# Row maxima of an attention unit: transposed by VectorE in squares of 32 instead of by a matmul

## The chip, the cores and the metric

The kernel runs on one core of a Trainium2 chip. The metric is the device time of one execution in microseconds (us); "before" and "after" are each given as the median over several executions. A core has a matrix engine (TensorE, PE in the profile; its weight loads are listed apart as PEld), a vector engine (VectorE, DVE), an engine for activation functions (ScalarE, ACT), a general one (GpSimd, POOL) and a queue engine (SyncE, SP), which here issues all transfers. SBUF is the core's working memory of 128 partitions; PSUM holds eight banks into which matmuls write; DRAM is the memory outside the core.

## The reference

```python
xn = _layernorm(x)                                   # x: 1 x 2048 x 512, fp32
qkv = (xn @ wqkv)                                    # 32 heads of 16
scores = einsum("bhqd,bhkd->bhqk", q, k) * 16 ** -0.5
p = softmax(scores)                                  # over 2048 keys
s = einsum("bhqk,bhkd->bhqd", p, v) ... @ wo         # attention, 512 x 512 output weights
h = relu(xn @ w1 + b1) ** 2                          # 512 -> 1792
g = silu(h @ w2 + b2)                                # 1792 -> 512
out = x + s * g
```

Everything is fp32. The softmax of the reference subtracts the maximum of each score row before the exponential. The kernel does that too, and the change is in how these maxima get to the place where they are subtracted.

## The kernel before

fp32 operands are split into a high and a low part, and a product is the sum of three matmuls. The 32 heads are taken four at a time (eight "quads"), and the 2048 queries in four chunks of 512. One quad with one chunk is a *unit*; there are 32 units (`NU`). For a unit the kernel does two things, far apart in time.

*Maxima.* `max_mm` (L288 to L310) computes, for one head, 128 queries and 512 keys, the scores in one PSUM bank (matmul L300), and VectorE reduces the bank to one column of maxima (L308). A unit has 4 heads x 4 blocks of 128 queries x 4 chunks of 512 keys, that is 64 such matmuls and 64 reductions. The banks come from the pool `pm`, which has three: a matmul can start when the reduction of the matmul three places before it has let go of its bank. When the 64 are done, `max_end` (L314) reduces the 64 columns to 16 (L326), one per head and block of queries, partitions being queries: a tile `m4` of 128 x 16. It notes the unit in `late`, due two steps on.

*Shift.* `shift_due` (L330) calls `shift(u)` (L334) when the unit is due. The maxima have to become rows: for head and query block a row of 128 values. Before, a matmul against the identity does it (L336, a PE transpose of 128 x 16 into 16 x 128), which takes one of the three `pm` banks. VectorE reads the bank twice: it writes the negated maxima as a high part (L338) and the remainder as a low part (L339) into the tile `sh` of 16 partitions. The inner function `keep` writes the two halves to the DRAM tile `sh_d[u]` by two transfers (L345), and `back`, through `shift_rows` (L367, transfer L368), reads them into rows 48 and 49 of each half of the unit's query tiles `qe`. The key tiles have ones in these rows, so the score matmul itself subtracts the maximum.

*Use.* `exp_mm` (L1245) makes the scores of 128 keys by 512 queries (matmul L1258) and ScalarE takes the exponential (L1264); `pv_step` multiplies with the values (matmuls L375, in `pv_mm`) and accumulates over the 16 blocks of keys of a unit. One block of keys of one unit is a *step*; there are 512 steps. When a unit ends, `evac` starts a chain of small works over the next steps, among them three GpSimd instructions one behind the other (L413, L414, L415 in `evac_norm`).

The MLP (`mlp_tasks`) and the output product are generators whose matmuls are laid between those of the attention: `slot` (L1298) and `long_slots` (L1337) write out, matmul by matmul, which follows which. Two matmuls of 64 rows each run side by side in the upper and the lower half of the array, so their order alternates between the halves. The L336 transpose and the L375 matmuls use all 128 rows. From L1417 on the order on all engines is that of the program text: on VectorE the reductions of the maxima come in the order of their matmuls, and the shift's instructions stand between two of them, at the end of a slot. SP too takes its transfers in the order of the text and stands still when the next one has to wait; `keep` is put one step, `back` at least two steps behind `shift` (`later`, L181, due by `run_waiting`, L185). `back` is due 14 steps ahead of the first step of its unit or, where the shift comes after that, two steps behind the shift. In the stage before the loop (`first`, L1104) TensorE, VectorE, ScalarE and GpSimd keep the order of the text.

The loop has three kinds of stretches around a shift: slots of a single step (2.9 us each), pairs of steps in which long blocks of MLP matmuls stand (5.5 us a pair, `long_slots` in its first form), and the same blocks cut at each step (2.1 and 3.6 us in turn, its second form). The rows of the next sections are from these.

Of the kernel before, what the change touches and what calls it, by code (L numbers as in the profile page):

```python
# [8 lines left out]
F32 = mybir.dt.float32  # L9
F32R = mybir.dt.float32r  # L10
AF = mybir.ActivationFunctionType
ALU = mybir.AluOpType
# [4 lines left out]
P = 128  # L17
# [9 lines left out]
NU = NQ * 4  # L27
# [13 lines left out]
def kernel(  # L41
# [11 lines left out]
    nc = tc.nc  # L53
# [3 lines left out]
    dram = ctx.enter_context(tc.tile_pool(name="dram", bufs=1, space=DRAM))  # L57
    q_d = [dram.tile([2, P, S], F32, name=f"q_d{m}") for m in range(4)]
    k_d = [dram.tile([2, P, S], F32, name=f"k_d{m}") for m in range(4)]
    sh_d = [dram.tile([4, 2, 512], F32, name=f"sh_d{u}") for u in range(NU)]  # L60
    r_d = [dram.tile([4, 512], F32, name=f"r_d{u}") for u in range(NU)]
    on_d = [dram.tile([2, P, S], F32, name=f"on_d{k}") for k in range(KO)]
    xn_d = dram.tile([2, P, KO, S], F32, name="xn_d")
# [5 lines left out]
    ident = const.tile([P, P], F32, name="ident")  # L69
# [26 lines left out]
    with ExitStack() as ph:  # L96
        kp = ph.enter_context(tc.tile_pool(name="kp", bufs=1))
        sp = ph.enter_context(tc.tile_pool(name="asp", bufs=2))
        pe = ph.enter_context(tc.tile_pool(name="pe", bufs=3, space=PSUM))
        pm = ph.enter_context(tc.tile_pool(name="pm", bufs=3, space=PSUM))  # L100
# [27 lines left out]
        mxs = {}  # L128
# [52 lines left out]
        def later(n, fn):  # L181
            waiting.append((now[0] + n, fn))
# [147 lines left out]
        def shift_due():  # L330
            if late and late[0][0] <= now[0]:
                shift(late.pop(0)[1])

        def shift(u):  # L334
            pt = pm.tile([P, 512], F32, name="pm_t")
            nc.tensor.transpose(pt[:16, :P], mxs[u], ident)  # L336
            sh = sp.tile([16, 2, P], F32R, name="sh", bufs=1)
            nc.vector.tensor_scalar(sh[:, 0], pt[:16, :P], -1.0, None, op0=ALU.mult)  # L338
            nc.vector.scalar_tensor_tensor(  # L339
                sh[:, 1], pt[:16, :P], -1.0, sh[:, 0].bitcast(F32),  # L340
                op0=ALU.mult, op1=ALU.subtract,
            )
            def keep():
                for i in range(2):
                    nc.sync.dma_start(  # L345
                        sh_d[u][:, i, :].rearrange("h (b n) -> h b n", n=P),
                        sh[:, i, :].bitcast(F32),
                    )

            def back():  # L350
                for p in range(2):
                    for i in range(2):
                        shift_rows(u, p, i)

            if in_loop:
                later(1, keep)
                later(max(2, 16 * u - 14 - now[0]), back)
            else:
                keep()
                if u < 2:  # L360
                    back()
                else:
                    waiting.append((16 * u - 14, back))
# [3 lines left out]
        def shift_rows(u, p, i):  # L367
                    nc.sync.dma_start(  # L368
                        qes[u][p].rearrange("(j r) n -> j r n", r=64)[:, 48 + i].bitcast(F32),
                        sh_d[u][2 * p : 2 * p + 2, i],  # L370
                    )

        def pv_mm(po, qd, kb, pts):
# [747 lines left out]
        for i in range(NT + 3):  # L1121
# [21 lines left out]
            if i >= 3 and (i - 3) % 4 == 3:  # L1143
                c = (i - 3) // 4
# [31 lines left out]
        b = 0  # L1176
# [10 lines left out]
        while len(rest) > 1:  # L1187
# [42 lines left out]
            if b % 2 and b < 16:  # L1230
                c, i = divmod(b // 2, 2)
# [266 lines left out]
```

## Time and profile before

| | us |
|---|---|
| median of three executions | 1663.76 (1663.0 to 1664.24) |
| the profiled execution's own time | 1665.93 |
| its span in the trace | 1664.2 |
| TensorE busy (98%) | 1630.7 |
| VectorE busy (81%) | 1342.1 |
| ScalarE busy (71%) | 1185.6 |
| GpSimd busy (31%) | 511.3 |

A row of the timeline has the start in us, the length in us, the engine, the line, the operation, the tile written and those read, the shapes, and how many like instructions are merged; in brackets stands how long the engine had been idle and what ended the wait. A row of the groups has the line, the engine, the operation, tiles and shapes, the count, then the busy time in us and the mean length of one in ns, then the idle time before them. A row of the chain of work that ended last has start, length, engine, tile and line. The rows of one source line give the shortest, the median and the longest length in ns. The granted TensorE clock was 0.996 of full speed.

### The profile page before, as it was taken

The page shows a single profiled execution, that of the slowest core. Times are in us where ns is not written, and L with a number is a line of the kernel's source. Part 1 is how long each engine was busy: PE and PEld are TensorE (multiplying, and loading weights), DVE is VectorE, ACT ScalarE, POOL GpSimd, SP SyncE. Part 2 cuts the span into 40 slices and gives each one's busy share as a digit, 9 for nine tenths or more (in the row PEclk, how much of TensorE's full clock was granted, in tenths as well). Part 3 has the DMA queues.
Part 4 walks back from the last instruction along what each step waited for, and adds up shares of the span by engine and source line. Part 5 has one row for each costly group of instructions (what it writes and reads, how often), then busy time and mean ns, then how long its engine had stood idle before and what let it go on. Part 6 is the DMA issues. An engine that isn't in the chain of part 4 may idle for free.

```text
span 1664.2 us, 35916 instructions
## 1 busy us (share of the span) xinstructions
PE 1630.7 (98%) x13674; PEld 983.9 (59%) x13674; DVE 1342.1 (81%) x2300; ACT 1185.6 (71%) x2344; POOL 511.3 (31%) x533
## 2 busy tenths in 40 slices
PE   6999999999999999999999999999999999999998
PEld 4898666456656665665565456555654565544455
DVE  6499988788787878777878888888888888887823
ACT  6221477678777877787777777777777777776784
POOL 4435567513312221231133113301321224113224
PEclk9999999999999999999999999999999999999999
DMA  8577555426322622353243424342432442144344
GB/s 285 167 227 250 178 177 157 125 65 174 86 87 76 165 70 81 95 140 79 78 119 97 96 72 131 102 105 71 122 98 71 104 129 73 47 115 128 118 140 140
DMA packets 152980, 201.22 MB, mean 121 GB/s; under 512 B 50856, under 2 KB 70824, under 8 KB 151272
## 3 DMA queue, kind: packets, MB, share of 16 engines
q1 hardware_dynamic: 152808, 198.93, 41.4%
q8 instruction: 108, 1.77, 0.4%
q14 instruction: 64, 0.52, 0.1%
HBM read 144.58 MB, written 53.99 MB: 119 GB/s over the span
## 4 chain that ended last, share of the span: by engine, by line
PE 92%; DVE 3%; DMA 2%; SPq 1%; ACT 1%; issue 0%; POOL 0%; DVEq 0%; ACTq 0%; POOLq 0%
PE po L375 29%; PE pd_t L234 16%; PE pm_t L300 16%; PE se L1258 15%; PE pd_t L202 5%; PE se L1016 3%; DVE mx L308 2%; PE pd_t L775 2%; PE se L967 2%; PE pd_t L1016 1%; PE po L1016 1%; DMA sm<-ot 1%; SPq L132 1%; PE pm_t L336 1%; DMA wv<-in_A_wqkv_dram 0%; DMA oc<-on_d 0%
## 5 line engine op out<-in xcount | busy, mean ns | idle before, releaser
L308 DVE TENSOR_REDUCE mx<-pm_t 128x1 f32<-128x512 f32 x2048 | 1266.1, 682 | 229.4 <-PE pm_t L300 116.9
L1264 ACT ACTIVATE pt<-se 128x512 f32<-128x512 f32 x1750 | 926.3, 614 | 237.9 <-PE se L1258 169.4
L300 PE MATMUL pm_t<-ka,qm 64*128 64x512 f32 x2048 | 779.6, 416 | 8.3 <-DVE mx L308 7.2
L1258 PE MATMUL se<-qe,ka 64*128 64x512 f32 x2016 | 746.4, 416 | 0.0
L375 PE MATMUL po<-pt,v 128*32 128x512 f32 x3564 | 526.2, 604 | 0.0
L300 PEld LDWEIGHTS pm_t<-ka,qm 64*128 64x128 f32 x2048 | 359.5, 184 | 217.9 <-DVE mx L308 203.0
L1258 PEld LDWEIGHTS se<-qe,ka 64*128 64x128 f32 x2016 | 353.7, 184 | 114.0 <-ACT pt L1264 67.5
L234 PEld LDWEIGHTS pd_t<-xc,w1s 64*128 64x128 f32 x2352 | 295.6, 187 | 44.1 <-issue 41.9
L234 PE MATMUL pd_t<-xc,w1s 64*128 64x256 f32 x2352 | 320.3, 285 | 0.0
L234 PE MATMUL pd_t<-w2t,hT 64*128 64x512 f32 x936 | 252.5, 405 | 0.0
L375 PE MATMUL po<-ex,v 128*32 128x512 f32 x532 | 213.2, 602 | 0.0
L1264 ACT ACTIVATE ex<-se 128x512 f32<-128x512 f32 x266 | 159.0, 614 | 44.9 <-PE se L1258 20.9
L234 PEld LDWEIGHTS pd_t<-w2t,hT 64*128 64x128 f32 x936 | 160.2, 184 | 44.1 <-issue 35.2
L375 PEld LDWEIGHTS po<-pt,v 128*32 128x32 f32 x3564 | 89.3, 108 | 155.3 <-issue 138.1
L549 POOL TENSOR_TENSOR r<-r 128x512 f32<-128x512 f32 x49 | 51.0, 1041 | 321.4 <-ACT r L546 321.4
L413 POOL TENSOR_TENSOR ot<-ot,hl 128x512 f32<-128x512 f32 x31 | 39.8, 1285 | 225.4 <-DMA hl<-r_d 179.2
L568 POOL TENSOR_TENSOR u<-u,b_t 128x512 f32<-128x512 f32 x16 | 20.6, 1288 | 287.1 <-ACT u L567 230.0
L202 PE MATMUL pd_t<-w2t,hT 64*128 64x512 f32 x408 | 106.6, 393 | 2.0 <-POOL w2t L80 1.2
L202 PEld LDWEIGHTS pd_t<-w2t,hT 64*128 64x128 f32 x408 | 73.1, 185 | 11.8 <-POOL w2t L80 1.6
L775 PE MATMUL pd_t<-wot,oc 64*128 64x512 f32 x258 | 74.3, 410 | 0.2 <-DMA oc<-on_d 0.2
L81 POOL TENSOR_TENSOR hT<-r,hT 128x512 fp32r<-128x512 f32 x56 | 72.3, 1292 | 4.7
L1016 PE MATMUL se<-xT,wr_t 64*128 64x512 f32 x312 | 66.3, 392 | 0.0
(131 smaller groups left out, 1202.9 us busy)
## 6 DMA issues: line engine op xcount, KB each, us to landing
w1s<-w_d SPq DMA_DIRECT2D x196, 256.0 KB
qm<-q_d SPq DMA_DIRECT2D x384, 32.0 KB
qe<-q_d SPq DMA_DIRECT2D x384, 32.0 KB
ka<-k_d SPq DMA_DIRECT2D x96, 128.0 KB
xn_d<-xT SPq DMA_DIRECT2D x8, 1024.0 KB
k_d<-hl SPq DMA_DIRECT2D x32, 256.0 KB
q_d<-hl SPq DMA_DIRECT2D x32, 256.0 KB
xc<-xn_d SPq DMA_DIRECT2D x16, 512.0 KB
```

Of the source, the lines that this page charges most:

```text
L81: (lo or nc.gpsimd).tensor_tensor(dst[1], raw, dst[0].bitcast(F32), op=ALU.subtract)
L202: mm = nc.tensor.matmul(out_, lh(r), rh(r), start=first_ and lane == 0, stop=last_ and lane == 1, skip_group_check=True,)
L234: mm = nc.tensor.matmul(out_, lh(r), rh(r), start=first_ and lane == 0, stop=last_ and lane == 1, skip_group_check=True,)
L300: nc.tensor.matmul(ps, qms[u][p][64 * j : 64 * j + 64, qb * P : (qb + 1) * P], kas[qd, p][64 * j : 64 * j + 64, kc * 512 : (kc + 1) * 512] ...
L308: return nc.vector.tensor_reduce(mxs[u][:, c, kc : kc + 1], ps, axis=AX.X, op=ALU.max)
L375: nc.tensor.matmul(po[32 * j : 32 * j + 32, :], vs[qd][:, (4 * kb + j) * VW : (4 * kb + j) * VW + 32], pts[j], start=(kb == 0), stop=(kb = ...
L413: nc.gpsimd.tensor_tensor(ot, ot, hl[:, 1].bitcast(F32), op=ALU.mult)
L549: nc.gpsimd.tensor_tensor(r, r, r, op=ALU.mult)
L775: inst = nc.tensor.matmul(ps[lane], oc[r, a, n, ts_], wot[r, b, n], start=m == 0 and (lane == 0 or wide), stop=m == kos and (lane == 1 or ...
L1016: inst = nc.tensor.matmul(out_, lh(r), rh(r), start=first_ and lane == 0, stop=last_ and lane == 1, skip_group_check=True,)
L1258: nc.tensor.matmul(se, kas[qd, j // 2][b : b + 64, kb * P : (kb + 1) * P], qes[u][j // 2][b : b + 64, :], start=True, stop=True,)
L1264: return nc.scalar.activation(pts[j], se, AF.Exp, scale=0.25)
```

## The change

The three instructions of VectorE now read the maxima where they lie, 128 partitions by 16, and write the high and the low part side by side into a tile of 128 x 32. A transpose on VectorE then turns each square of 32 partitions by 32 columns of it: partition 32 b + r of the new tile `sq` holds 32 queries of block b for row r, r being 16 times the part plus the head and query block. One transfer writes the whole tile to DRAM, whose layout is now 32 rows of 128 queries. `shift_rows` reads the same 2 x 512 values as before at their new place. The matmul L336 and its bank in `pm` are gone; the tiles `sh` and `sq` have two buffers each, where `sh` had one.

```diff
-    sh_d = [dram.tile([4, 2, 512], F32, name=f"sh_d{u}") for u in range(NU)]
+    sh_d = [dram.tile([32, P], F32, name=f"sh_d{u}") for u in range(NU)]
...
         def shift(u):
-            pt = pm.tile([P, 512], F32, name="pm_t")
-            nc.tensor.transpose(pt[:16, :P], mxs[u], ident)
-            sh = sp.tile([16, 2, P], F32R, name="sh", bufs=1)
-            nc.vector.tensor_scalar(sh[:, 0], pt[:16, :P], -1.0, None, op0=ALU.mult)
+            sh = sp.tile([P, 2, 16], F32R, name="sh")
+            nc.vector.tensor_scalar(sh[:, 0], mxs[u], -1.0, None, op0=ALU.mult)
             nc.vector.scalar_tensor_tensor(
-                sh[:, 1], pt[:16, :P], -1.0, sh[:, 0].bitcast(F32),
-                op0=ALU.mult, op1=ALU.subtract,
-            )
+                sh[:, 1], mxs[u], -1.0, sh[:, 0].bitcast(F32), op0=ALU.mult, op1=ALU.subtract
+            )
+            sq = sp.tile([P, 32], F32, name="sq")
+            nc.vector.transpose(sq, sh.rearrange("p i c -> p (i c)").bitcast(F32))
+
             def keep():
-                for i in range(2):
-                    nc.sync.dma_start(
-                        sh_d[u][:, i, :].rearrange("h (b n) -> h b n", n=P),
-                        sh[:, i, :].bitcast(F32),
-                    )
+                nc.sync.dma_start(sh_d[u].rearrange("r (b q) -> b r q", q=32), sq)
...
         def shift_rows(u, p, i):
                     nc.sync.dma_start(
                         qes[u][p].rearrange("(j r) n -> j r n", r=64)[:, 48 + i].bitcast(F32),
-                        sh_d[u][2 * p : 2 * p + 2, i],
+                        sh_d[u][16 * i + 8 * p : 16 * i + 8 * p + 8].rearrange(
+                            "(j b) q -> j (b q)", j=2
+                        ),
                     )
```

## The prediction

> **What bounds the kernel now.** I read the page first: span, busy shares and the chain of work that ended last.
>
> ```profile
> span 1664.2 us, 35916 instructions
> PE 1630.7 (98%) x13674; PEld 983.9 (59%) x13674; DVE 1342.1 (81%) x2300; ACT 1185.6 (71%) x2344; POOL 511.3 (31%) x533
> ...
> PE 92%; DVE 3%; DMA 2%; SPq 1%; ACT 1%; issue 0%; POOL 0%; DVEq 0%; ACTq 0%; POOLq 0%
> ```
>
> TensorE carries 92% of the chain and is busy nearly always. Time that its queue loses is time of the span; time of another engine counts only where TensorE has to wait for it. Next I asked for the line that goes, L336.
>
> ```profile
> L336 PE MATMUL pm_t<-ident,m x32: 276/277/278, 115.5 to 1590.5; 128*16 128x128 f32 x32
> ...
>   DVE mx L308: 13.5, 31
> ```
>
> There are 32 transposes of 0.277 us, one per unit, with 13.5 us of waits for a bank or for the matmuls ahead in front of them. What one costs in its slot is read from the chain and from TensorE's timeline, as the distance from one group of L375 matmuls to the next, with a transpose in the slot and without.
>
> ```profile
> 442.29 1.85 PE po L375 x16
> 448.05 1.85 PE po L375 x16
> 453.51 1.85 PE po L375 x16
> ```
> ```profile
> 345.73 1.06 PE L375 MATMUL po<-pt,v 128*32 128x512 f32 x8
> ...
> 348.81 1.06 PE L375 MATMUL po<-pt,v 128*32 128x512 f32 x8
> ...
> 351.70 1.07 PE L375 MATMUL po<-pt,v 128*32 128x512 f32 x8
> ...
> 1029.83 0.63 PE L375 MATMUL po<-pt,v 128*32 128x512 f32 x3
> ...
> 1032.35 0.62 PE L375 MATMUL po<-ex,v 128*32 128x512 f32 x1
> ...
> 1035.92 1.07 PE L375 MATMUL po<-pt,v 128*32 128x512 f32 x8
> ...
> 1038.05 0.62 PE L375 MATMUL po<-pt,v 128*32 128x512 f32 x1
> ```
>
> Transposes stand at 447.77, 348.61 and 1032.14. Long pairs: 448.05 - 442.29 = 5.76 against 5.46, so 0.30 us each. Single steps: 348.81 - 345.73 = 3.08 against 2.89, so 0.19. Cut blocks: 1032.35 - 1029.83 = 2.52 against 1038.05 - 1035.92 = 2.13, so 0.39. Going along the trace I count 9 units in long pairs, 6 in single steps, 14 in cut blocks, two ahead of the loop and one at its end.
>
> Then VectorE behind the transposes, and the maxima matmuls that follow there.
>
> ```profile
> 1033.20 0.27 DVE L338 TENSOR_SCALAR sh<-pm_t 16x128 fp32r<-16x128 f32 x1
> 1033.50 0.28 DVE L339 SCALAR_TENSOR_TENSOR sh<-pm_t,sh 16x128 fp32r<-16x128 f32 x1
> 1033.88 3.08 DVE L308 TENSOR_REDUCE mx<-pm_t 128x1 f32<-128x512 f32 x5
> ...
> 450.41 1.89 DVE L308 TENSOR_REDUCE mx<-pm_t 128x1 f32<-128x512 f32 x3 [0.99 <-PE se L1258]
> ```
> ```profile
> 1033.35 0.50 PE L300 MATMUL pm_t<-ka,qm 64*128 64x512 f32 x1
> ...
> 1035.31 0.40 PE L300 MATMUL pm_t<-ka,qm 64*128 64x512 f32 x1
> ```
>
> In a long pair VectorE is idle for 0.99 us behind the shift. In a cut block (and in the single steps alike) it is not: it ends the shift at 1033.78 and starts reducing at 1033.88, when the matmul of 1033.35 has just ended. Five reductions follow in 3.08 us. The second is over near 1033.88 + 2 x 0.62 = 1035.1, and the fifth matmul, which needs its bank, starts at 1035.31. So after a shift VectorE has 0.1 us to spare and the banks some 0.1 to 0.2: what holds VectorE there holds TensorE.
>
> **The change part by part.** *The matmul and its bank go.* By the distances 9 x 0.30 + 6 x 0.19 + 14 x 0.39 = 9.3 us, and some 0.8 us for the other three units: 10 us if nothing else bound. But in the cut blocks the next maxima matmuls come 0.39 us sooner while VectorE is free no sooner (next point), and the fifth then waits for its bank. Only the 0.1 us that VectorE had to spare remains of the 0.39. (In the single steps that and the banks' 0.1 cover the 0.19.) So without any trouble it is 9 x 0.30 + 6 x 0.19 + 14 x 0.1 + 0.8 = 6.0 us.
>
> *Three VectorE instructions instead of two.* None of the new forms is in the trace; their lengths come from the nearest ones.
>
> ```profile
> L339 DVE SCALAR_TENSOR_TENSOR sh<-pm_t,sh 16x128 fp32r<-16x128 f32 x32 | 8.9, 278 | 1.1
> ...
> L399 DVE RECIPROCAL sm<-sm 128x16 f32<-128x16 f32 x31 | 7.5, 244 | 8.9 <-DMA sm<-ot 8.9
> ...
> L1061 DVE RECIPROCAL rstd<-rstd 128x1 f32<-128x1 f32 x16 | 2.1, 133 | 1.2 <-ACT rstd L1056 1.2
> ...
> L849 DVE TENSOR_TENSOR thl<-tot,thl 128x256 fp32r<-128x256 f32 x2 | 0.8, 421 | 0.2 <-ACT thl L847 0.2
> L874 DVE TENSOR_SCALAR ot<-po 128x512 f32<-128x512 f32 x1 | 0.7, 693 | 5.2 <-PE po L375 5.2
> ...
> L828 DVE TENSOR_SCALAR rs<-tsm 128x512 f32<-128x512 f32 x1 | 0.4, 427 | 0.0
> ```
>
> From 256 to 512 elements an instruction grows by 693 - 421 = 272 ns, or 1.06 ns per element, on a base of some 150 ns. That makes 0.16 us for the scalar instruction on 16 elements, 0.17 for the one with two inputs and 0.15 + 0.03 = 0.18 to 0.21 for the transpose of 32 columns. With two gaps of 0.03, as between L338 and L339, it is 0.58 us, as long as the two of before (1033.20 to 1033.78). Each of the three is bounded by 0.133 (one element) and 0.278: 0.46 to 0.89 in all, so -0.1 to +0.3 us for each unit; over the 20 units without idle VectorE time -2 to +6 us. I take nothing.
>
> *Where they read.* L338 and L339 read PSUM; the new ones read SBUF alone, the second with two inputs there. At the end of the trace stand the only VectorE instructions with two SBUF inputs that meet a working GpSimd:
>
> ```profile
> 1656.62 0.69 DVE L866 TENSOR_TENSOR g<-pd_t,g 128x512 f32<-128x512 f32 x1
> 1657.35 1.13 DVE L867 TENSOR_TENSOR g<-g,ts 128x512 f32<-128x512 f32 x1
> ...
> 1659.71 1.26 DVE L867 TENSOR_TENSOR g<-g,xr 128x512 f32<-128x512 f32 x1
> ```
> ```profile
> 1656.63 1.30 POOL L867 TENSOR_TENSOR g<-g,ts 128x512 f32<-128x512 f32 x1 [7.21 <-DVE g L866]
> 1659.15 1.26 POOL L867 TENSOR_TENSOR g<-g,xr 128x512 f32<-128x512 f32 x1 [1.23 <-DVE g L866]
> ```
>
> GpSimd's two end at 1657.93 and 1660.41. VectorE's L867, begun meanwhile, end at 1658.48 and 1660.97, both 0.55 us later: 512 elements at 1.06 ns. They did not run at half rate, they stood still until GpSimd was done. L866, with one input in PSUM, ran beside GpSimd at its usual 0.69, and L849, with two SBUF inputs and no GpSimd, at its usual 0.42. So the new L339 waits for a GpSimd instruction under way. The new L338 has one input, but L828 shows the scalar instruction from SBUF at 427 ns where from PSUM it takes 693: it reads two elements at a time, and I take it to wait as two inputs do. The transpose I take to be free. GpSimd in turn is held for the 0.16 or 0.17 us of such an instruction; only stores of SP wait for it.
>
> Is GpSimd at work at those moments? In the unit shown:
>
> ```profile
> 1032.75 0.62 POOL L414 TENSOR_SCALAR hl<-ot 128x512 fp32r<-128x512 f32 x1
> 1033.46 1.29 POOL L415 TENSOR_TENSOR hl<-ot,hl 128x512 fp32r<-128x512 f32 x1
> ```
>
> At 1033.20 L414 runs until 1033.37. The scalar instruction then takes 0.16, L415 is next in line at 1033.52 and runs 1.29, until 1034.81; only then the second goes, then the transpose, done near 1035.2 instead of 1033.78: held by 1.44 us. I did this for each shift of the 20 units without idle VectorE time. In twelve GpSimd is busy nearly throughout the 1.80 us from the start of L338; one answer groups these twelve, a second the other eight:
>
> ```profile
> sum 21.60, POOL 19.27; mean POOL 1.61
> ```
> ```profile
> sum 14.40, POOL 0.95; mean POOL 0.12
> ```
>
> The held times of the twelve, one by one, come to 19.1 us, a mean of 1.59, as the busy time says; those of the eight to 0.2. A unit held by h costs TensorE about h - 0.1 against now, its saving being swallowed in the same wait: 19.1 - 1.2 = +17.9 us. The eight others: 6 cut blocks at -0.1 and 2 single steps at -0.19, -1.0. The nine long pairs -2.7, with 0.7 back where GpSimd holds two of them beyond their idle time. The three at the ends: -0.3. Sum +14.6 us. Of the twelve, some will slip through where GpSimd pauses for 0.1 us between two instructions; one or two fewer make it +12.
>
> The Trainium skill, page "SBUF — State Buffer", section "SBUF: two separate sides", says that VectorE's two-port and two-input instructions and GpSimd's share a port pair, held by one for a whole instruction. By that rule both new instructions wait, +14.6 us; by the rows alone only the wait of the second is shown, which is the second case below.
>
> *The transfers.* Two become one, of 128 pieces of 128 bytes instead of 32 of 512.
>
> ```profile
> 1033.50 1.32 SPq L345 DMA_DIRECT2D sh_d<-sh  x2
> ```
> ```profile
> PE pd_t L775 <- DMA oc<-on_d: 0.2, 1, 0.2
> ```
>
> SP saves one issue of 0.66 us, or nothing if the one takes as long as two. Behind it stand weight loads and the four reads of `back`, and SP will stand still until the transpose is done, so up to 1.5 us longer in twelve units. The cover is distance: the rows are read 14 steps ahead, some 40 us, and in the whole trace TensorE waited 0.2 us in the loop for a transfer. I take nothing; without that cover the hold of 1.5 us would stand a second time, twelve times, +18. The Trainium skill, page "DMA: Bandwidth & Descriptors", section "Specifications", asks for 512 bytes or more, below which a write becomes read-modify-write; no row here prices it.
>
> **The rivals.** *Only the instruction with two inputs waits* (or GpSimd cannot slip in between the two). Then only what is left of one GpSimd instruction counts, some 5 us over the 20 units by the same reading, against the 6.0 saved, with some of the saving swallowed: -2 to +3, about 1664. For it speaks that no row shows a one-input instruction waiting; against it L828's rate.
>
> *Nothing waits, and it is faster.* If so small an instruction gets through at once, the 6.0 us remain: 1658; with VectorE at its short bound 1654. For it speaks that the reciprocals L399, in SBUF with one input, keep their 244; against it both L867. It decides from a mean hold of about 0.5 us per unit held, below which the twelve cost less than the rest saves.
>
> *The landing of the small pieces binds,* so that `back` and the loads behind it come late: the price above, on top, some 1685 to 1695. Little speaks for it.
>
> **How the numbers follow.** The profiled execution took 1665.9, its span 1664.2; the median is 1663.8, 2.2 below, and I put the sum on the median: 1663.8 + 12 = 1676, +0.7%. Both instructions held: 0.55, by itself 1669 to 1683 (hold of half to all, VectorE lengths +-). Only one held: 0.22. Nothing: 0.15. Landing or lengths at their upper bound: 0.08. The range leaves out most of the last two: 1660 to 1684. A measurement of this kernel tells 0.2%, or 3.3 us, from no change: slower 0.64, same 0.20, faster 0.16.
>
> **What would show it.** L336 gone and the long pairs at 5.46 throughout; the scalar and the two-input instruction of the shift with lengths from 0.16 to over 1.2 us, long exactly where GpSimd runs; in the cut blocks behind such shifts the 3.57 us slot grown by about as much, TensorE waiting for L308. Lengths of 0.2 us everywhere would make the prediction wrong and the kernel faster; a long transpose, or `qe` late, would make it slower for another reason.

## The result and the profile after

| | before | after |
|---|---|---|
| median, both on the same chip, 17 executions each | 1664.19 (1661.25 to 1667.32) | 1661.50 (1659.00 to 1663.07) |
| ratio with its 95% interval | | 0.9985 (0.9978 to 0.9992) |
| the profiled execution's own time | 1665.93 | 1662.81 |
| its span | 1664.2 | 1661.0 |

The change makes the kernel 0.15% faster, about 2.5 us; that is not zero by its interval, and it is inside the 0.2% that the prediction called no change. Forecast were 1676 us and slower. That 1661.5 lies inside the forecast range of 1660 to 1684 is luck: the range was that wide because it took in another case than the one forecast.

The page of after, with the span, the busy shares and the chain of work that ended last:

```profile
span 1661.0 us, 35806 instructions
...
PE 1625.6 (98%) x13642; PEld 983.6 (59%) x13642; DVE 1349.1 (81%) x2332; ACT 1187.8 (72%) x2344; POOL 510.9 (31%) x533
...
PE 93%; DVE 3%; DMA 2%; SPq 1%; ACT 0%; issue 0%; POOL 0%; DVEq 0%; ACTq 0%
```

TensorE has 32 matmuls less and is busy 5.1 us less; VectorE has 32 instructions more and is busy 7.0 us longer. TensorE still bounds the kernel. The rows of the tile `sh`, with the shortest, median and longest length in ns, and then the groups, with the busy time in us and the mean in ns, show what has grown:

```profile
L336 DVE TENSOR_SCALAR sh<-m x32: 109/168/1257, 116.7 to 1585.1; 128x16 fp32r<-128x16 f32 x32
L337 DVE SCALAR_TENSOR_TENSOR sh<-m,sh x32: 174/176/1219, 117.2 to 1585.6; 128x16 fp32r<-128x16 f32 x32
L341 DVE STREAM_TRANSPOSE sq<-sh x32: 211/211/214, 117.4 to 1586.9; 128x32 f32<-128x32 f32 x32
```
```profile
L336 DVE TENSOR_SCALAR sh<-m 128x16 fp32r<-128x16 f32 x32 | 12.0, 374 | 0.0
L337 DVE SCALAR_TENSOR_TENSOR sh<-m,sh 128x16 fp32r<-128x16 f32 x32 | 8.2, 255 | 1.1
```

The medians are 0.17, 0.18 and 0.21 us, and two of the three instructions are sometimes 1.2 us long. Whatever lies above the medians is time in which the instruction is held: 12.0 - 32 x 0.168 = 6.6 us for the scalar instruction and 8.2 - 32 x 0.176 = 2.6 us for the one with two inputs, 9.2 us over all 32 units. Over the 20 units in which VectorE has no idle time behind the shift, I added it up one by one: 6.2 us, 1.5 of them the two-input instruction's. The prediction had put 19.3 there.

Where a shift is not held, TensorE's slot has become shorter. First the chain in the long pairs (the shift stands at 392.94, between the second and the third row), then TensorE's timeline in a cut block whose shift stands at 984.28:

```profile
386.23 1.85 PE po L373 x16
391.71 1.85 PE po L373 x16
397.17 1.85 PE po L373 x16
```
```profile
980.91 1.07 PE L373 MATMUL po<-pt,v 128*32 128x512 f32 x8
...
983.04 0.62 PE L373 MATMUL po<-pt,v 128*32 128x512 f32 x1
...
986.79 0.62 PE L373 MATMUL po<-pt,v 128*32 128x512 f32 x1
```

Long pairs with a shift now take 5.46 like those without one. The cut block takes 2.13 ahead of the shift, where a transpose made it 2.52, and 3.75 behind it, where it was 3.57: of the 0.39 us about 0.18 comes back as a wait. I compared each unit's matmuls in both traces, from the step ahead of the shift to two steps behind it, and call the sum of these differences the ledger:

| units | predicted, us | ledger, us |
|---|---|---|
| 9 long pairs | -2.7 + 0.7 | -2.59 |
| 6 single steps | -0.19 each if quiet | -1.39 for five, +0.34 for the held one at 796 |
| cut blocks not held | -0.1 each | -1.15 for seven (-0.13 to -0.18 each) |
| cut blocks held | h - 0.1 each, twelve units (four of them single steps) with 19.1 in all | +2.56 for seven (+0.12 to +0.82 each) |
| the unit at the end | | -0.20 |
| sum | +14.6 | -2.43 |

The ledger accounts for the measured 2.5 us (0.8 of the spans' 3.2 lie at other steps). One of the five single steps, the unit at 301, is held longest of all, 1.46 us, and still shows a gain: its slot ahead of the shift took 4.61 us before and 2.87 now. That slot shrinks in e2 and e3 too, where the matmul transpose stays, so its gain is not the change's.

The 6.2 us of hold lie in the twelve units in which they were expected, but nine of these are held by 0.3 to 1.5 us and three by less than 0.1. The mean is 0.5 us, and 1.6 was forecast. That is the question that is left.

### The profile page after: what moved, and what is told of

Read it like the earlier page. It is cut to its first block, busy times and chain, and to the rows that moved or that the text cites. A ratio compares the mean times of both kernels' runs of the same rounds, so it can differ in the third digit from the quotient of the medians.

```text
span 1661.0 us, 35806 instructions
## 1 busy us (share of the span) xinstructions
PE 1625.6 (98%) x13642; PEld 983.6 (59%) x13642; DVE 1349.1 (81%) x2332; ACT 1187.8 (72%) x2344; POOL 510.9 (31%) x533
## 4 chain that ended last, share of the span: by engine, by line
PE 93%; DVE 3%; DMA 2%; SPq 1%; ACT 0%; issue 0%; POOL 0%; DVEq 0%; ACTq 0%
PE po L373 29%; PE pm_t L300 16%; PE pd_t L234 16%; PE se L1256 15%; PE pd_t L202 5%; PE se L1014 3%; DVE mx L308 2%; PE se L965 2%; PE pd_t L773 2%; PE pd_t L1014 1%; PE po L1014 1%; SPq L132 1%; DMA sm<-ot 0%; DMA xc<-xn_d 0%; DMA xt<-in_A_x_dram 0%; PE pm_t L807 0%
## 5 line engine op out<-in xcount | busy, mean ns | idle before, releaser
L411 POOL TENSOR_TENSOR ot<-ot,hl 128x512 f32<-128x512 f32 x31 | 39.9, 1286 | 220.9 <-DMA hl<-r_d 148.2
L81 POOL TENSOR_TENSOR hT<-r,hT 128x512 fp32r<-128x512 f32 x56 | 72.3, 1291 | 4.7
```

Source lines behind the costliest of these rows:

```text
L81: (lo or nc.gpsimd).tensor_tensor(dst[1], raw, dst[0].bitcast(F32), op=ALU.subtract)
L411: nc.gpsimd.tensor_tensor(ot, ot, hl[:, 1].bitcast(F32), op=ALU.mult)
```

## The experiments

**The two theories.** The prediction's mechanism was that VectorE stands still while a GpSimd instruction runs, once for the scalar and once more for the two-input instruction. The trace of after shows the first. Theory S: the hold is real, and what saves the time is that the second instruction stands close behind the first. A held instruction does its start-up during the wait and ends just behind GpSimd's end, and the next begins while GpSimd pauses for 0.1 us. Rival R: GpSimd just happens not to be at work at those moments, or a waiting VectorE has precedence, so that where the second instruction stands makes no difference. The unit that the prediction worked out, now at 1030, by the timeline of after:

```profile
1029.64 0.62 POOL L412 TENSOR_SCALAR hl<-ot 128x512 fp32r<-128x512 f32 x1
...
1030.07 0.23 DVE L336 TENSOR_SCALAR sh<-m 128x16 fp32r<-128x16 f32 x1
1030.33 0.18 DVE L337 SCALAR_TENSOR_TENSOR sh<-m,sh 128x16 fp32r<-128x16 f32 x1
1030.35 1.32 POOL L413 TENSOR_TENSOR hl<-ot,hl 128x512 fp32r<-128x512 f32 x1
```

L412 ends at 1030.26. The scalar instruction ends 0.04 us behind that, not 0.16, and the two-input instruction starts at 1030.33, by 0.02 us ahead of the GpSimd instruction that was to hold it for 1.29. The other kind of unit, at 892, where a GpSimd instruction has just begun when the shift comes:

```profile
891.29 1.29 POOL L413 TENSOR_TENSOR hl<-ot,hl 128x512 fp32r<-128x512 f32 x1
...
891.44 1.17 DVE L336 TENSOR_SCALAR sh<-m 128x16 fp32r<-128x16 f32 x1
...
892.64 0.18 DVE L337 SCALAR_TENSOR_TENSOR sh<-m,sh 128x16 fp32r<-128x16 f32 x1
```

GpSimd's ends at 892.58, the scalar instruction at 892.61. So a one-input instruction from SBUF does wait, for all that is left of GpSimd's. And a two-input one does, where it comes too late for the pause:

```profile
1167.78 0.16 DVE L336 TENSOR_SCALAR sh<-m 128x16 fp32r<-128x16 f32 x1
1167.84 0.62 POOL L412 TENSOR_SCALAR hl<-ot 128x512 fp32r<-128x512 f32 x1
1167.98 0.49 DVE L337 SCALAR_TENSOR_TENSOR sh<-m,sh 128x16 fp32r<-128x16 f32 x1
```

The pause is there only where GpSimd's next instruction needs the output of the last. In after, L412 starts 0.09 us behind L411 in each of 31 cases and L413 0.08 behind L412. L80, which begins another tile, starts 0.02 to 0.05 us *before* the end of the L81 ahead of it wherever it has nothing else to wait for (38 cases). So in the unit at 301 the second instruction is held again, right behind a scalar one that was held until 302.65:

```profile
302.59 0.63 POOL L80 TENSOR_SCALAR w2t<-ex 128x512 fp32r<-128x512 f32 x1
...
302.69 0.54 DVE L337 SCALAR_TENSOR_TENSOR sh<-m,sh 128x16 fp32r<-128x16 f32 x1
```

All runs, each against the kernel before on the same chip:

| kernel | what | median, us | before there, us | ratio (95%) |
|---|---|---|---|---|
| e1 | after, GpSimd's work two steps later | 1655.63 | 1665.13 | 0.9942 (0.9928 to 0.9956) |
| e2 | before, GpSimd's work two steps later | 1659.44 | 1665.13 | 0.9967 (0.9956 to 0.9979) |
| e3 | before, a second transpose on TensorE | 1666.36 | 1665.13 | 1.0008 (0.9997 to 1.0018) |
| e4 | after, VectorE does the transpose alone | 1651.64 | 1665.13 | 0.9922 (0.9907 to 0.9938) |
| e5 | after, GpSimd makes both parts early | 1653.05 | 1664.78 | 0.9931 (0.9919 to 0.9944) |
| e6 | after, the store in two | 1662.98 | 1664.78 | 0.9989 (0.9977 to 1.0001) |
| e7 | after, an independent instruction between the two | 1663.57 | 1664.78 | 0.9995 (0.9985 to 1.0004) |
| e8 | e4 with GpSimd's work later | 1649.27 | 1664.78 | 0.9911 (0.9898 to 0.9925) |
| e9 | after, a chained instruction between the two | 1672.01 | 1665.82 | 1.0038 (1.0026 to 1.0050) |
| e10 | e5 with GpSimd's work later | 1648.67 | 1665.82 | 0.9899 (0.9885 to 0.9913) |
| e11 | after, the chained instruction behind the two | 1666.69 | 1665.82 | 1.0007 (0.9998 to 1.0016) |

**e1 and e2: move GpSimd's work away from the shift.** The steps at which a unit's output is normalized come two steps later; in e1 on the kernel after, in e2 on the kernel before. These are the three GpSimd instructions L411 to L413, but also the transfer that brings their input and the one that stores their output. The last four units keep their steps.

```diff
-EVAC = (1, 4, 5, 7, 9, 12)
+EVAC = (1, 4, 5, 9, 11, 14)
```

> The changed kernel, but the broadcast of the reciprocals and with it GpSimd's three instructions of a unit's end come two steps later, so that they should not be at work when a shift comes. Nothing of VectorE's or TensorE's order is touched. Theory H (a shift is held by the rest of the GpSimd instruction under way, and that cost about 4 us of the 6 that the removed matmul gave): the scalar and the two-input instruction at 0.2 us or less in nearly all units of the later half, and the time about 4 us under the changed kernel, 1657 to 1658, or 0.996 of before. Rival L (the holds are taken up elsewhere; the gain is small because VectorE's three instructions are as long as the two of before and the banks bind): the lengths fall, the time stays at 1661 to 1662.

> The kernel before with the same move of GpSimd's three instructions. There the shift reads PSUM and does not meet GpSimd. H and L alike: no change, 1664 plus or minus 1.5. If it gains what the move gains in the changed kernel, the move itself and not the hold is the cause there.

The groups of e1:

```profile
L336 DVE TENSOR_SCALAR sh<-m 128x16 fp32r<-128x16 f32 x32 | 7.9, 246 | 0.0
L337 DVE SCALAR_TENSOR_TENSOR sh<-m,sh 128x16 fp32r<-128x16 f32 x32 | 7.8, 243 | 1.1
```

The held time falls from 9.2 to (7.9 - 5.4) + (7.8 - 5.6) = 4.7 us, in the 20 units from 6.2 to 2.2, and the cut blocks that are then free of GpSimd gain 0.16 to 0.23 each. So the long instructions come from GpSimd's work. The times alone would say too much: the same move makes the kernel before 5.7 us faster, though its shift is not held there: L339 takes 0.278 or 0.279 us in every unit of before, beside GpSimd or not. No change was expected of e2, 1664 plus or minus 1.5. In the ledger that gain stands at steps far from the shifts, behind waits for weights and for the sums of the softmax. The waits of before and then of e2, in all, times, longest:

```profile
POOL w2t L80 <- DMA ex<-in_B_w_dram: 9.0, 4, 8.1
...
DVE sm L399 <- DMA sm<-ot: 8.9, 4, 4.6
```
```profile
DVE sm L399 <- DMA sm<-ot: 9.0, 6, 2.4
...
POOL w2t L80 <- DMA ex<-in_B_w_dram: 5.4, 2, 3.9
```

The longest of each kind is half as long in e2. That these two account for the 5.7 us was not settled. Between e2 and e1, with the same move in both, the change is worth 0.25%, against 0.15% without it: in the expected direction, but within the two intervals.

**e3: what a transpose costs TensorE.** A second, unused transpose into the same bank.

```diff
             nc.tensor.transpose(pt[:16, :P], mxs[u], ident)
+            nc.tensor.transpose(pt[:16, P : 2 * P], mxs[u], ident)
```

> The kernel before with a second, unused matmul transpose of the same maxima into other columns of the same bank, ahead of the first: the price of TensorE's part alone, without another bank. If a transpose costs TensorE its 0.2 to 0.28 us in each of 32 slots, the time rises by 7 to 9 us, to 1671 to 1673. If the slots hide it, it stays near 1664.

```profile
1030.37 0.28 PE L336 MATMUL pm_t<-ident,m 128*16 128x128 f32 x1
...
1030.48 0.27 PE L337 MATMUL pm_t<-ident,m 128*16 128x128 f32 x1
```

The second follows 0.11 us behind the first, and the ledger gives 0.11 us per unit. So one more transpose behind the first costs 0.11 us, while the first costs 0.30, 0.19 or 0.39 in its slot. What the rest is, the change from the matmuls around it to the transpose and back or something else, no row here divides further. The time (+0.08%) cannot be told from no change; expected were 7 to 9 us, or none.

**e4: the same without the two instructions.** The reduction that ends a unit's maxima writes them negated and rounded into a tile whose other half is zero, and the shift is the transpose alone. The low part is left out.

```diff
+        neg = [const.tile([P, 32], F32R, name=f"neg{i}") for i in range(2)]
...
-                    nc.vector.tensor_reduce(m4, mxs[u], axis=AX.X, op=ALU.max)
+                    m4 = neg[u % 2]
+                    nc.vector.tensor_reduce(
+                        m4[:, :16], mxs[u], axis=AX.X, op=ALU.max, negate=True
+                    )
...
-            nc.vector.tensor_scalar(sh[:, 0], mxs[u], -1.0, None, op0=ALU.mult)
-            nc.vector.scalar_tensor_tensor(
-                sh[:, 1], mxs[u], -1.0, sh[:, 0].bitcast(F32), op0=ALU.mult, op1=ALU.subtract
-            )
-            nc.vector.transpose(sq, sh.rearrange("p i c -> p (i c)").bitcast(F32))
+            nc.vector.transpose(sq, mxs[u].bitcast(F32))
```

> The changed kernel with neither the scalar nor the two-input instruction: the reduction to 16 columns writes the negated maxima itself, rounded to the high part, and only the square transpose is left of the shift on VectorE. The low part is left out (its rows are zero), so the subtracted maximum is the rounded one, the same for all keys of a query. H: no hold anywhere, and with VectorE 0.4 us shorter at each shift the cut blocks get most of their 0.39 us: 4 us for the holds and 3 for the cut blocks, 1654 to 1655. L: only the 3 us for the shorter VectorE work, 1658 to 1659.

A cut block of e4, its shift at 1023.22:

```profile
1019.85 0.63 PE L373 MATMUL po<-pt,v 128*32 128x512 f32 x3
...
1021.98 0.62 PE L373 MATMUL po<-ex,v 128*32 128x512 f32 x1
```
```profile
L341 DVE STREAM_TRANSPOSE sq<-neg 128x32 f32<-128x32 f32 x32 | 6.3, 197 | 0.0
```

The transpose is never held, though GpSimd's work stands where it stood: 32 at a mean of 0.197. Long pairs gain 2.71 us in the ledger, the 14 cut blocks 5.38 (0.35 to 0.42 each), the quiet single steps 0.20 each. These are the prices of the transpose that the prediction read from the trace of before. That the cut blocks now gain all of the 0.39, and in after only 0.16, shows the other half too: with VectorE's shift at 0.58 us the saved time is swallowed by VectorE, with 0.20 it is not. These terms, some 9.5 us, are most of the 13.5 measured; the time is 2 to 3 us under the forecast. In the compared pair of traces 1.5 more stand at the unit at 301, which gains 1.4 us in e3 and 1.5 in e2 too and so not by this edit, and some 3 at the start and at steps far from the shifts. What these 3 are stays open.

**e5: the split on GpSimd.** The reduction negates, and GpSimd makes the high and the low part right behind it, two steps ahead of the shift, which is the transpose alone.

```diff
-                    nc.vector.tensor_reduce(m4, mxs[u], axis=AX.X, op=ALU.max)
+                    nc.vector.tensor_reduce(m4, mxs[u], axis=AX.X, op=ALU.max, negate=True)
...
+                    sh = shs[u] = sp.tile([P, 2, 16], F32R, name="sh")
+                    split((sh[:, 0], sh[:, 1]), m4)
...
-            nc.vector.tensor_scalar(sh[:, 0], mxs[u], -1.0, None, op0=ALU.mult)
-            nc.vector.scalar_tensor_tensor(
-                sh[:, 1], mxs[u], -1.0, sh[:, 0].bitcast(F32), op0=ALU.mult, op1=ALU.subtract
-            )
+            sh = shs.pop(u)
```

> The changed kernel with the scalar and the two-input instruction moved to GpSimd and two steps ahead, directly behind the reduction to 16 columns (which writes the negated maxima); VectorE's shift is the square transpose alone, the low part is kept. H: VectorE meets no hold and is as short as with the negated reduction alone; cut blocks -0.39, single steps -0.2, long pairs -0.3 us each against before, the time 1652 to 1654. If GpSimd's own queue makes the transpose late, it is 1656 or more, and VectorE shows waits for GpSimd at the transpose.

```profile
L81 POOL TENSOR_TENSOR sh<-m,sh 128x16 fp32r<-128x16 f32 x32 | 7.1, 223 | 2.7
L80 POOL TENSOR_SCALAR sh<-m 128x16 fp32r<-128x16 f32 x32 | 6.6, 207 | 112.8 <-DVE m L327 112.8
L340 DVE STREAM_TRANSPOSE sq<-sh 128x32 f32<-128x32 f32 x32 | 6.3, 196 | 1.0 <-POOL sh L81 1.0
```

13.7 us of work move to an engine with a share of 31%, and VectorE waits for it once, 1.0 us. GpSimd's 112.8 us of idle time ahead of it do not show at the shifts: the ledger is e4's (long pairs -2.76, cut blocks -5.45).

**e6: two stores.** The store is cut in two; its pieces keep their 128 bytes.

```diff
-                nc.sync.dma_start(sh_d[u].rearrange("r (b q) -> b r q", q=32), sq)
+                for b in range(0, 4, 2):
+                    nc.sync.dma_start(
+                        sh_d[u].rearrange("r (b q) -> b r q", q=32)[b : b + 2],
+                        sq[32 * b : 32 * b + 64],
+                    )
```

> The changed kernel with its one store of 128 pieces cut into two of 64 pieces each: SP issues as often as before the change. If the transfers lie beside the work, as the prediction took it, nothing moves: 1661 to 1662. If SP's issue was part of the gain, it gives back up to 32 x 0.5 us in the stretches where SP is late.

0.9989 against 0.9985: one more issue on SP in each unit changes nothing that can be told. What the size of the pieces does, this run does not test. For that stands the trace of after: none of TensorE's matmuls that read `qe` waits for a transfer there, so the stores and what comes behind them lie beside the work, as predicted.

**e7: a gap between the two, first try.** An independent reduction of the maxima between the scalar and the two-input instruction. By theory S the second misses GpSimd's pause, by R nothing happens.

```diff
+        gap_t = const.tile([P, 1], F32, name="gap_t")
...
             nc.vector.tensor_scalar(sh[:, 0], mxs[u], -1.0, None, op0=ALU.mult)
+            nc.vector.tensor_reduce(gap_t, mxs[u], axis=AX.X, op=ALU.max)
```

> The changed kernel with a small unused reduction of VectorE (16 columns to one, about 0.16 us, one input) between the scalar and the two-input instruction. Theory S (the two-input instruction escapes the next GpSimd instruction only because it starts within GpSimd's pause of some 0.08 us): now GpSimd's next instruction starts first wherever there is one; the two-input instruction grows to 0.6 to 1.3 us in units 14, 15, 17, 19 and 21 and by 0.7 in two of the first units, some 5 us in the units without idle time, and 20 units get 0.14 us longer, 3 us: 1668 to 1670. Rival R (VectorE goes ahead of a waiting GpSimd whatever the pause): only the 3 us, 1664 to 1665, and no new long two-input instruction.

```profile
985.72 0.16 DVE L337 TENSOR_SCALAR sh<-m 128x16 fp32r<-128x16 f32 x1
985.79 0.16 DVE L338 TENSOR_REDUCE gap_t<-m 128x1 f32<-128x16 f32 x1
985.91 0.18 DVE L339 SCALAR_TENSOR_TENSOR sh<-m,sh 128x16 fp32r<-128x16 f32 x1
```

It tells nothing. The three starts lie within 0.19 us: the independent instruction runs inside the time in which the second waits for the first anyway, so there was no gap. With two exceptions (1.27 and 0.33 us) no two-input instruction became long that was not so in after.

**e8: e4 with the move of e1.** The diff is those of e4 and e1 together.

> The negated reduction (without the low part, as there) and the later move of GpSimd's three instructions together. The first gave 13 us against before, the second 5.7 in the kernel before. If the second's gain lies in other places than the shifts, as its ledger of steps says, they add up: 1645 to 1647.

0.9911, against 0.9922 for e4: the move adds 0.1% here, where it gave 0.33% to the kernel before and gives 0.32% to e5 (e10, below). Expected were 1645 to 1647 us, and 1649.27 came out. With intervals of 0.15% to either side the three may be the same gain or not. In e2 and e10 it is clear of the intervals, and no shift is held there, so this gain is not the shift's.

**e9 and e11: a gap that is one, and its control.** A copy that needs the first instruction's output and that the next one reads, made by a reduction with one input over single elements. In e9 it stands between the scalar and the two-input instruction, in e11 behind both.

```diff
             nc.vector.tensor_scalar(sh[:, 0], mxs[u], -1.0, None, op0=ALU.mult)
+            hi = sp.tile([P, 16], F32, name="hi")
+            nc.vector.tensor_reduce(
+                hi, sh[:, 0].bitcast(F32)[:, :, None], axis=AX.X, op=ALU.max
+            )
             nc.vector.scalar_tensor_tensor(
-                sh[:, 1], mxs[u], -1.0, sh[:, 0].bitcast(F32), op0=ALU.mult, op1=ALU.subtract
+                sh[:, 1], mxs[u], -1.0, hi, op0=ALU.mult, op1=ALU.subtract
             )
```
```diff
-            nc.vector.transpose(sq, sh.rearrange("p i c -> p (i c)").bitcast(F32))
+            both = sp.tile([P, 32], F32, name="both")
+            nc.vector.tensor_reduce(
+                both, sh.rearrange("p i c -> p (i c)").bitcast(F32)[:, :, None],
+                axis=AX.X, op=ALU.max,
+            )
+            nc.vector.transpose(sq, both)
```

> The changed kernel with a one-input reduction (a copy of the 16 high values, about 0.16 us) that waits for the scalar instruction and for which the two-input instruction waits, so that 0.2 us instead of 0.03 lie between the two. Theory S (the two-input instruction escapes GpSimd's next instruction only because it is ready within GpSimd's pause of some 0.08 us): behind every scalar instruction that was held and has a next GpSimd instruction, the two-input instruction now takes 0.6 to 1.3 us; in the changed kernel that was so in units 14, 15, 17, 19 and 21. Per such unit in the cut blocks and single steps up to 1.2 us more, with the 0.2 us that all of them get longer 6 to 9 us in all: 1667 to 1670. Rival R (VectorE is served ahead of a GpSimd instruction that waits): no new long two-input instruction, 0.2 us for 20 units, 1664 to 1665.

> The control of the run with the gap: the same kind of reduction stands behind the two-input instruction, ahead of the transpose, so VectorE's shift is 0.2 us longer in the same way, but the two-input instruction stays close behind the scalar one. S and R alike: two-input instructions as short as in the changed kernel, 20 units up to 0.2 us longer, 1664 to 1666.

One unit in both, the one at 894, first of e9, then of e11. In both the shift comes while GpSimd's second instruction runs, and the scalar one is held for less than 0.1 us:

```profile
893.79 0.62 POOL L416 TENSOR_SCALAR hl<-ot 128x512 fp32r<-128x512 f32 x1
...
894.21 0.23 DVE L336 TENSOR_SCALAR sh<-m 128x16 fp32r<-128x16 f32 x1
894.47 0.17 DVE L338 TENSOR_REDUCE hi<-sh 128x16 f32<-128x16 f32 x1
894.49 1.28 POOL L417 TENSOR_TENSOR hl<-ot,hl 128x512 fp32r<-128x512 f32 x1
894.67 1.13 DVE L341 SCALAR_TENSOR_TENSOR sh<-m,hi 128x16 fp32r<-128x16 f32 x1
```
```profile
893.95 0.19 DVE L336 TENSOR_SCALAR sh<-m 128x16 fp32r<-128x16 f32 x1
894.17 0.18 DVE L337 SCALAR_TENSOR_TENSOR sh<-m,sh 128x16 fp32r<-128x16 f32 x1
894.19 1.32 POOL L418 TENSOR_TENSOR hl<-ot,hl 128x512 fp32r<-128x512 f32 x1
```

In e11 the two-input instruction starts 0.02 us ahead of GpSimd's third and takes 0.18. In e9 the copy stands at its place, GpSimd's third starts 0.02 us behind the copy, and the two-input instruction, 0.20 us later than it would have been, lasts until GpSimd is done (895.77) and 0.03 us more. The copy, a reduction over single elements, runs beside GpSimd at its usual 0.17. In TensorE's slots this unit loses 1.02 us against before in e9 and 0.05 in e11. The groups of e9, then of e11:

```profile
L341 DVE SCALAR_TENSOR_TENSOR sh<-m,hi 128x16 fp32r<-128x16 f32 x32 | 14.0, 439 | 1.1
...
L336 DVE TENSOR_SCALAR sh<-m 128x16 fp32r<-128x16 f32 x32 | 9.5, 298 | 0.0
L338 DVE TENSOR_REDUCE hi<-sh 128x16 f32<-128x16 f32 x32 | 5.4, 170 | 1.1
```
```profile
L336 DVE TENSOR_SCALAR sh<-m 128x16 fp32r<-128x16 f32 x32 | 9.8, 307 | 0.0
L337 DVE SCALAR_TENSOR_TENSOR sh<-m,sh 128x16 fp32r<-128x16 f32 x32 | 8.6, 269 | 1.1
L342 DVE TENSOR_REDUCE both<-sh 128x32 f32<-128x32 f32 x32 | 6.0, 186 | 1.1
```

The two-input instruction is held for 14.0 - 5.6 = 8.4 us in e9 and for 8.6 - 5.6 = 3.0 in e11, the scalar one for 4.1 and 4.4. The same work at another place: 5.1 us more held time, and 0.31% more of the whole, 5.2 us; the two intervals do not meet. The ledgers of the loop's shifts, +6.8 and +2.1 us, differ by 4.7. Rival R would have them alike. In e9 the two-input instruction is held by 0.1 to 1.0 us in twelve of the 20 units, the same twelve in which the prediction expected it in after, and in e11 in four. The kernel of e9 is slower than before by 0.38%.

**e10: the version that beats both.** The split on GpSimd (e5) and its output work two steps later (e1).

> The split on GpSimd two steps ahead together with the later move of GpSimd's three instructions: the fastest form that keeps the low part. The first gave 11.5 us against before, the move 5.5 in the kernel before and 2.5 on top of the negated reduction. If the move's gain lies in waits for transfers elsewhere: 1648 to 1651.

0.9899, that is 1.0% or 17 us faster than before, and about 14 us better than the change alone.

## Why the prediction was wrong

**Right: what bounds, and the price of the matmul.** TensorE's 0.30, 0.19 and 0.39 us for each slot, read as distances in the trace of before, came back in e4 and e5 as 0.30, 0.20 and 0.39. Reading the slot was needed: the instruction's 0.277 us is neither these prices nor the 0.11 that a second one costs in e3.

**Right: the swallowing in the cut blocks.** Predicted was 0.1 us left of 0.39, measured 0.13 to 0.18, and e4 shows that VectorE's 0.58 us is what swallows the rest. A held cut block was to cost its hold less 0.1; the seven were held by 3.9 us and cost TensorE 2.56, their hold less 0.19 each. The three instructions are 0.17, 0.18 and 0.21 us long where they are not held; predicted 0.16, 0.17 and 0.18 to 0.21, from neighbours of other shapes.

**Right: who waits for whom.** Both new instructions stand still while a GpSimd instruction runs, the one-input scalar form too, for which no row of before existed. The transpose does not, as the prediction took it, and neither does a plain reduction. The Trainium skill, page "SBUF — State Buffer", section "SBUF: two separate sides", has a VectorE instruction that runs in a two-port mode or has two SBUF inputs and a GpSimd instruction take a shared port pair in turns, each for its whole length; the trace agrees, with 1.17 us for an instruction of 0.17. TensorE's waits for VectorE grew as such a hold makes them: in all, times and longest, of before and then of after:

```profile
PE pm_t L300 <- DVE mx L308: 7.2, 9, 4.1
```
```profile
PE pm_t L300 <- DVE mx L308: 11.2, 16, 4.9
```

The seven more stand 1.6 to 2.7 us behind held shifts and come to 3.4 us. The longest wait, 4.1 and 4.9, stands in both traces far from any shift, at 1528.60 and 1525.95.

**Wrong: the size of the hold.** The step that failed is in "Where they read": "The scalar instruction then takes 0.16, L415 is next in line at 1033.52 and runs 1.29, until 1034.81; only then the second goes". It does not take 0.16 behind GpSimd's end, it takes 0.03 to 0.04, as if its start-up were done during the wait. And the next GpSimd instruction is not there at once; it starts 0.08 to 0.09 us behind the end of the last where it needs its output, as the two rows of L414 and L415 say (1033.37 and 1033.46). The prediction named this pause, but took only one or two of the twelve units, 2.6 us, off for it.

In after the scalar instruction was held in 15 of the 32 units. In six of them no further GpSimd instruction began within 1 us, in six the second instruction slipped into the pause, and in three (at 301, 1399 and 1585) it was held again by an instruction that GpSimd started without a pause. So mostly one hold counts where I had counted two, and of that one only what was left of GpSimd's instruction: 6.2 us in place of 19.3. With the end at 0.03 and the pause put in, the rows of L338 and of GpSimd in before give an estimate of 5.4 us of hold for the twelve units in place of 19.1. e9 against e11 shows that this is the cause: moving the second instruction by 0.2 us brings the second hold back.

The rows for it were quoted. By the growth that the prediction worked out, 512 elements take 0.55 us on a base of 0.15; L867 ended 0.55 behind GpSimd's end, so the base was already missing there. I had used that row for whether it waits and not for how it ends. For 16 elements the same row gives 16 x 1.06 ns = 0.02 us, and most units would have had one partial hold in the sum.

**The rivals.** By its time the result is nearest to the second case ("or GpSimd cannot slip in between the two", about 1664, -2 to +3 us); the words in brackets are what happened in six units, and its 5 us of hold are near the 6.2 measured. Its first half is not so: the scalar instruction carries 4.7 of the 6.2 us. "Nothing waits" (1658) falls by the long instructions. The landing of small pieces falls by the trace of after, in which no matmul waits for the rows in `qe`. The Trainium skill, page "DMA: Bandwidth & Descriptors", section "Specifications", asks for pieces of at least 512 bytes; no run here changes the size of the pieces alone. (For the cover the prediction read TensorE's wait of 0.2 us for a transfer; its weight loads waited another 0.4 once, at 200.8.)

**What stays open.** Why moving the output work two steps later is worth 5.7 us to the kernel before, and what the 3 us of e4 are that lie far from the shifts. Open is also how far the moment of the GpSimd work against the shift varies between executions of one kernel, as one trace of each was kept. In these the work follows the landing of a transfer (`hl`), and the scalar instruction of one unit, at 891 to 894, takes 1.17 us in after and 0.19 in e11.

## What to carry to other kernels

Before VectorE work is moved from PSUM to SBUF, see what GpSimd does at those moments, and count for each held instruction only what is left of GpSimd's. Then see whether GpSimd's next instruction needs the output of the last: in the pause before it a second VectorE instruction 0.03 us behind the first got through here, one 0.2 us behind did not, and where GpSimd's work was independent there was no pause. If such an instruction stands where an engine waits, use a form that is not held (here a reduction that negates, and the square transpose) or hand the small work to GpSimd itself, early enough that nobody waits. And price a matmul by the distances of its slot, with and without it: here 0.19 to 0.39 us, where a second one costs 0.11.

## What was not expected of the hardware

- A held VectorE instruction ends 0.03 us behind GpSimd's end with 16 elements (892.58 and 892.61), with 512 elements 0.55 behind it: as if its start-up overlapped the wait.
- GpSimd leaves 0.08 to 0.09 us between two dependent instructions and none between two independent ones (they overlap by 0.02 to 0.05). An instruction of VectorE that starts in the pause goes ahead of the next one of GpSimd, which then takes 1.32 us instead of 1.29.
- An independent VectorE instruction between two dependent ones is free: in e7 the three start within 0.19 us, where the two alone start 0.20 apart.
- The transpose of 32 x 32 squares, 128 x 32 in all, takes 0.21 us right behind the instruction that makes its input and 0.197 otherwise, and GpSimd never held it.
